# Three small shifts in a hand-written schedule: partial-result stores one slot sooner, the x chunks of block 2 two slots later, the first num burst one slot later

## The chip, the cores and the metric

The kernel runs on one core of a Trainium2 chip. The metric is the device time of one execution in microseconds. Three runs of the kernel before gave 513.34, 508.83 and 507.54 us; the median is 508.83 us.

The core has a matrix engine (PE, whose weight loads are listed as PEld), a vector engine (DVE), a scalar engine (ACT), a general-purpose engine (POOL) and a sync engine (SP), each with its own in-order queue of instructions, and 16 DMA engines that move data between device memory and the on-chip buffers. Nearly all transfers of this kernel are issued from SP's queue.

## The reference

One input x of 2048 rows by 512 feeds two branches, which a gate per row mixes:

```
g   = sigmoid((x * gate_w).sum(-1))
a   = linear attention of x: q, k, v = x @ wqkv, 32 heads of 16
      phi(y) = concat(softmax(y @ w_phi), softmax(-y @ w_phi))    for q and k
      kv = phi(k)^T v,  z = phi(k) summed over the rows
      o  = phi(q) kv / (phi(q) z + 1e-6),  a = o @ wo
b   = relu(x @ w1 + b1)^2 @ w2 + b2                                F = 1792
out = g * a + (1 - g) * b
```

## The kernel before

**Numbers.** Every large product is made of three matmuls on numbers that are split into a high and a low half (names ending in h and l: `xh`, `xl`, `w1h`, `w1l`, `hh`, `hl`, `oh`, `ol`). A split is one copy on ACT, which makes the high half, and one subtraction on DVE, which makes the low half (`split`, L65 to L71). `mm3` (L73 to L77) issues the three matmuls of a product; so L75, L76 and L77 are the lines of nearly all matmuls.

**Two sweeps of the feed-forward branch (FFN).** The rows of x are four blocks of 512. The 14 chunks of the hidden width are done in two sweeps of seven chunks. One step t is one chunk for one block: `do_up(t + 2)` makes 12 matmuls into a bank `u`, ACT and DVE make `hh` and `hl` of it (`hidden`, L453), and `down` makes 12 matmuls that add into the four accumulators `d`. After the seven steps of a block in sweep 0, DVE (L812) turns the four accumulators into four tiles `row`, and SP stores them to `part` in device memory (L817); sweep 1 reads them back and adds its own half.

**The attention branch in the gaps.** In sweep 0 the keys and values are made, two row chunks at a time (tiles `kx`, `ky`, `kz`; p1 to p7), and summed up (`kvps`, `kvs`). In sweep 1 the queries follow (`q`, `q_phi`, `transposed`), then for each pair of row chunks a burst of 32 small matmuls, `numer` (banks `num0`, `num1`, L420), then `attended` (bank `att`), whose matmuls take the split of num (`oh`, `ol`) as an operand.

**The fold of wq.** w_phi is multiplied into wq on the chip: `foldq_load` (slot 16) loads four tiles of wqT into `row` tiles (L200) and w_phi into a stage tile; `fold("q")` (L202) is a burst of 128 small matmuls (L209) in the middle of the `down` of step 9, whose results DVE transposes (L224, into `wqin`) and SP stores (`wqm`, L234). The burst writes four banks in turn: the two `u` banks and the two attention banks, of which one was `kz` (read last by DVE into `vext`) and one was `ky` (read last by DVE into `k`, L564).

**What sets the order.** `at(slot, f)` puts a call into a table; there are two slots to a step. Slot 2t runs ahead of `do_up(t + 2)`, slot 2t + 1 between it and the `down` of step t. A scheduler then orders each engine's queue from that program order, with priorities (`tc.high_priority`) and a few forced orders (`tc.issue_after`); every queue is fixed when the program is built. The pool of `row` tiles has six buffers, which the rows of the partial results, of wqT and of the sums of x (`rows_make`, POOL) share; a tile that takes over a buffer waits until the last user is done with it, for a partial result until its store has landed. On SP each transfer also waits for the one that was issued eight before it on the same queue.

**x.** `x_fetch(b)` loads the four chunks of block b (L161, tiles `xin`), `x_ready(b, k)` splits them (L67 on ACT, L70 on DVE) and `x_save` stores the halves for sweep 1.

Of the kernel before, what the change touches and what calls it, by code (L numbers as in the profile page):

```python
# [37 lines left out]
def tile_gated_mix(ctx: ExitStack, tc: tile.TileContext, xT, xn, wqT, wkT, wphi, wv, wo, w1, b1, w2, b2, gw, out):  # L38
    nc = tc.nc
# [33 lines left out]
    def mm3(o, a, b, sa, sb, first, last, **kw):  # L73
        (ah, al), (bh, bl) = a, b
        nc.tensor.matmul(o, ah[:, sa], bh[:, sb], start=first, stop=False, **kw)  # L75
        nc.tensor.matmul(o, ah[:, sa], bl[:, sb], start=False, stop=False, **kw)  # L76
        return nc.tensor.matmul(o, al[:, sa], bh[:, sb], start=False, stop=last, **kw)  # L77
# [10 lines left out]
    def row():  # L88
        return work.tile([P, D], F32, tag="row", name="row", bufs=6)
# [112 lines left out]
    def fold(nm):  # L202
        wph, t = st["wphi"], st["wT", nm]
        pss = [ps_u.tile([P, 512], F32, tag="u", name=f"fold{nm}{r}") for r in range(2)]
        pss += [p.tile([P, 512], F32, tag="s", name=f"fold{nm}") for p in banks]

        def mm(g, r, q):
            rows, cols = slice(32 * r, 32 * r + 32), slice(g * P + 32 * r, g * P + 32 * r + 32)
            return nc.tensor.matmul(pss[r][32 * q:32 * q + 32, g * P:(g + 1) * P], wph[rows, cols],  # L209
                                    t[g][rows, :].rearrange("r (k q i) -> r k q i", q=4, i=32)[:, :, q, :],  # L210
                                    start=True, stop=True, skip_group_check=True)


        todo = [(g, r, q) for g in range(NK) for q in range(4) for r in range(4)]
        with ExitStack() as stack:
            for i, x in enumerate(todo):
                st["up"] = mm(*x)
                if i < 4:
                    stack.enter_context(tc.issue_after(st["up"].ins))
        w = work.tile([P, 2, 4, NG, 32], F32, tag="phiT", name=f"w{nm}in", bufs=1).rearrange(  # L220
            "p u r g s -> p (u r g s)").rearrange("p (k g r s) -> p k g r s", k=NK, g=NK, r=4)
        for r in range(4):
            with tc.high_priority(offset=AHEAD):
                st["turn"] = nc.vector.transpose(w[:, :, :, r, :].rearrange("p k g s -> p g k s"),  # L224
                                                 pss[r].rearrange("p (g k i) -> p g k i", g=NK, i=32))
        st["w", nm] = [w[:, k].rearrange("p g r s -> p (g r s)") for k in range(NK)]
# [255 lines left out]
    def down(t, c, dps):  # L482
        sw, b, i = work_list[t]
        end = i == NFH - 1 or t == last - 2 and c == NC - 1
        st["down"] = mm3(dps[c], hid[t], down_w[sw * NFH + i], slice(c * P, (c + 1) * P), ALL, i == 0, end)
# [180 lines left out]
    def at(slot, f, *a):  # L666
        steps.setdefault(int(slot), []).append(lambda: f(*a))
# [40 lines left out]
    for b in range(NB):  # L708
        for c in range(NC):
            s = b * SL + 2 * c if b else 7 + c  # L710
            at(s, gate_load, b * NC + c)
            at(s + 2, gate_dot, b * NC + c)
        at(b * SL + 12, gates, b)
        at(b * SL + 15, x_save, b)
        if b < NB - 1:
            at((5, 17, 31)[b], x_fetch, b + 1)
            for k in range(NK):
                at((7, 20, 34)[b] + k // 2, x_ready, b + 1, k)
    base = (NB - 1) * SL
    at(46, foldq_fetch)  # L720
    for k in range(NK):
# [10 lines left out]
    for p in range(NB * NC // 2):  # L732
        n, s = 2 * p, 54 + 6 * p + 2 * (p > 0)
        q, late = divmod(n, NC)[0], p == NB * NC // 2 - 1
        t = s + 12 - late + 2 * (p == 0)
        at(t, finish, n, n % NC)
        at(t + 1, finish, n + 1, n % NC + 1)
        for c in range(2):
            at(s + 2 * c, do_q, NB + q, n + c, n % NC + c)
            at(s + 2 * c + 2 * (p == 0), do_q_scaled, n + c, n % NC + c)  # L740
        at(t - 2, do_n, p)
    for b, slot in enumerate((46, 63, 72, 82)):
        at(slot, do_x, NB + b)

# [3 lines left out]
    def do_up(t):  # L748
        if t < len(work_list):
            sw, b, i = work_list[t]  # L750
            fc = sw * NFH + i
            hid[t] = up(fc, st["x", sw * NB + b], up_w[fc], t == FOLD_AT[0] + LAG)
# [4 lines left out]
    for t, (sw, b, i) in enumerate(work_list):  # L757
        with tc.issue_after(st["turn"].ins) if t == FOLD_AT[0] + 1 else nullcontext():
            for f in steps.get(2 * t, ()):
                f()  # L760


        with tc.issue_after(st["down"].ins) if 0 < t <= LAG else nullcontext():
            fold("k") if t == 1 else do_up(t + LAG)
        for f in steps.get(2 * t + 1, ()):
            f()
        if i == 0:
            dps = [ps_d.tile([P, 512], F32, tag="d", name=f"d{c}") for c in range(NC)]


        now = () if t == last - 1 else (t - 1, t) if t == last else (t,)

        with tc.issue_after(st["up"].ins) if t < LAG else nullcontext():
            for c in range(NC):
                if t == last and c == NC - 1:
                    break
                if t == FOLD_AT[0] and c == NC // 2:
                    with tc.issue_after(st["down"].ins):
                        fold("q")
                    with tc.issue_after(st["turn"].ins):  # L780
                        st["rest"]()
                with tc.issue_after(st["up"].ins) if t == FOLD_AT[0] and c >= NC // 2 else nullcontext():
                    for u in now:
                        down(u, c, dps)
        if t == 1:
            with tc.issue_after(st["down"].ins):
                do_up(t + LAG)
        if t == last:
            ends = [ps_u.tile([P, 512], F32, tag="u", name=f"end{j}") for j in range(2)]
            sc = slice((NC - 1) * P, NC * P)  # L790
            for j, s in enumerate(halves):
                for u in now:
                    st["down"] = mm3(ends[j][:, s], hid[u], down_w[NFH + u - last + NFH - 1], sc, s, u == now[0], u == last)
        if i < NFH - 1:
            continue
        for c in range(NC):
            n = b * NC + c
            done = ("f", n) in st
            if sw == 0:
                o = row()  # L800
                nc.scalar.activation(o, b2b, AF.Copy, scale=rest[:, n:n + 1])
            else:
                if not done:
                    st["f", n] = row()
                    nc.sync.dma_start(st["f", n], part[n])
                o = st["f", n]
            dst = part[n] if sw == 0 else out[n * P:(n + 1) * P, :]
            final = t == last and c == NC - 1
            for d, ss in [(dps[c], (ALL,))] + ([(ends[0], halves[:1]), (ends[1], halves[1:])] if final else []):
                for s in ss:  # L810
                    with tc.high_priority(offset=AHEAD):
                        nc.vector.scalar_tensor_tensor(o[:, s], d[:, s], rest[:, n:n + 1], o[:, s], ALU.mult, ALU.add)  # L812
            if final:
                for e, s in zip((nc.sync, nc.scalar), halves):
                    e.dma_start(dst[:, s], o[:, s])
            elif sw == 0 and b < NB - 1:
                at(2 * t + 3 + c // 2, lambda *a: nc.sync.dma_start(*a), dst, o)  # L817
            elif sw == 0 or done:
                nc.sync.dma_start(dst, o)

# [46 lines left out]
```

## Time and profile before

| | |
|---|---|
| median of three runs | 508.83 us |
| the profiled execution, its own time | 508.95 us |
| its span, first to last instruction | 507.2 us |
| DVE busy | 404.3 us (80%) |
| ACT busy | 254.3 us (50%) |
| POOL busy | 75.5 us (15%) |
| DMA, all queues | 84.79 MB, mean 167 GB/s |
| granted PE clock, mean | 1.000 |

The span is 1.8 us shorter than the execution's own time. A row of the timeline has the start in us from the first instruction, the length in us, the engine, the line of the kernel, the operation, the tile written and the tiles read, and how many instructions were joined into the row; a bracket at its end gives the idle time ahead of it and who ended it. SPq is SP's queue of transfers. In the chain of waits a row has a start, a length and what the end of the kernel waited for in that time.

### The profile page before, as it was taken

To read this page: it belongs to the slowest core of one execution; us is meant where nothing else is said; L and a number is where in the kernel's file an instruction comes from. 1 tells how busy PE (TensorE), PEld (TensorE's weight loads), DVE (VectorE), ACT (ScalarE), POOL (GpSimd) and SP (SyncE) were. 2 spreads that over 40 slices of the span, in tenths; PEclk is the share of its full clock that TensorE was granted. 3 is DMA by queue.
4 is the path that set the end of the run, shared out by engine and by line. 5 is a ranking of instruction groups with operands and counts; after the bars stand their busy time and mean duration, and the time that the engine had idled before them with its cause. 6 is when DMAs were issued, how large, how long until landed. Compare 5 with 4: busy or idle time off the path is not lost.

```text
span 507.2 us, 9518 instructions
## 1 busy us (share of the span) xinstructions
PE 500.7 (99%) x3616; PEld 404.2 (80%) x3616; DVE 404.3 (80%) x642; ACT 254.3 (50%) x433; POOL 75.5 (15%) x77
## 2 busy tenths in 40 slices
PE   9999999899999999999999999999999999999997
PEld 4878888688888888888888878788787878788876
DVE  5979995797879777887889998978789677798724
ACT  6598573454654557273664744343525353433530
POOL 5303020202050000000004131202121212102100
PEclk9999999999999999999999999999999999999999
DMA  8998777886556756936658252223153221032102
GB/s 297 336 359 291 244 261 251 280 300 188 177 199 232 239 175 200 298 111 177 187 161 310 75 191 54 89 52 95 37 179 100 83 79 44 7 101 81 41 23 83
DMA packets 52437, 84.79 MB, mean 167 GB/s; under 512 B 8104, under 2 KB 14504, under 8 KB 52392
## 3 DMA queue, kind: packets, MB, share of 16 engines
q1 hardware_dynamic: 52072, 83.79, 51.2%
q8 instruction: 28, 0.46, 0.4%
q10 hardware_dynamic: 288, 0.39, 0.2%
q14 instruction: 17, 0.14, 0.1%
q0 software_dynamic: 32, 0.01, 0.0%
HBM read 56.37 MB, written 21.50 MB: 154 GB/s over the span
## 4 chain that ended last, share of the span: by engine, by line
PE 94%; ACT 3%; DMA 3%; issue 0%; DVE 0%; SPq 0%
PE u L75 9%; PE d L75 9%; PE d L77 9%; PE d L76 9%; PE u L76 9%; PE u L77 9%; PE q L75 3%; PE q L76 3%; PE att L77 3%; PE q L77 3%; PE att L75 3%; PE att L76 3%; PE ky L75 2%; PE ky L77 2%; PE ky L76 2%; PE kvps L374 2%
## 5 line engine op out<-in xcount | busy, mean ns | idle before, releaser
L455 ACT ACTIVATE r<-u,b1c 128x512 f32<-128x512 f32 x56 | 38.4, 685 | 146.8 <-PE u L77 146.7
L383 POOL TENSOR_TENSOR ez<-e,z 128x512 f32<-128x512 f32 x32 | 41.8, 1328 | 278.2 <-ACT e L354 160.4
L75 PE MATMUL d<-w2h,hh 128*128 128x512 f32 x160 | 62.6, 391 | 0.0
L77 PE MATMUL d<-w2h,hl 128*128 128x512 f32 x160 | 62.3, 389 | 0.0
L76 PE MATMUL d<-w2l,hh 128*128 128x512 f32 x160 | 62.3, 389 | 0.0
L75 PE MATMUL u<-xh,w1h 128*128 128x512 f32 x152 | 59.6, 392 | 0.1
L76 PE MATMUL u<-xl,w1h 128*128 128x512 f32 x152 | 59.2, 389 | 0.0
L77 PE MATMUL u<-xh,w1l 128*128 128x512 f32 x152 | 59.2, 389 | 0.0
L359 DVE TENSOR_REDUCE sm<-e 128x64 f32<-128x1024 f32 x32 | 38.9, 1214 | 19.3 <-ACT e L354 19.3
L460 DVE TENSOR_TENSOR hl<-r,hh 128x512 fp32r<-128x512 f32 x56 | 38.5, 687 | 13.1 <-ACT hh L459 13.1
L407 ACT ACTIVATE phiT<-tb 32x256 f32<-32x256 f32 x64 | 26.5, 413 | 32.1 <-DVE tb L401 31.4
L354 ACT ACTIVATE e<-e 128x1024 f32<-128x1024 f32 x32 | 33.8, 1055 | 12.6 <-DVE e L352 12.3
L459 ACT ACTIVATE hh<-r 128x512 fp32r<-128x512 f32 x56 | 35.3, 630 | 1.5
L456 ACT ACTIVATE r<-r 128x512 f32<-128x512 f32 x56 | 35.2, 629 | 1.3
L75 PEld LDWEIGHTS d<-w2h,hh 128*128 128x128 f32 x160 | 30.0, 188 | 6.6 <-issue 0.4
L77 PEld LDWEIGHTS d<-w2h,hl 128*128 128x128 f32 x160 | 30.0, 188 | 6.3
L76 PEld LDWEIGHTS d<-w2l,hh 128*128 128x128 f32 x160 | 30.0, 188 | 6.2
L272 POOL TENSOR_TENSOR row<-xin 128x256 f32<-128x256 f32 x16 | 17.3, 1089 | 116.6 <-DVE S4ol L70 27.4
L75 PEld LDWEIGHTS u<-xh,w1h 128*128 128x128 f32 x152 | 28.5, 188 | 7.6 <-issue 0.8
L77 PEld LDWEIGHTS u<-xh,w1l 128*128 128x128 f32 x152 | 28.5, 188 | 6.1
L76 PEld LDWEIGHTS u<-xl,w1h 128*128 128x128 f32 x152 | 28.5, 188 | 5.8
L385 DVE TENSOR_REDUCE dz<-ez 128x64 f32<-128x1024 f32 x16 | 19.4, 1210 | 9.4 <-POOL ez L383 9.3
(544 smaller groups left out, 1161.1 us busy)
## 6 DMA issues: line engine op xcount, KB each, us to landing
in<-in_w SPq DMA_DIRECT2D x66, 256.0 KB, 3.3
phiT<-tb SPq DMA_DIRECT2D x192, 32.0 KB, 1.9
w2l<-lkept SPq DMA_DIRECT2D x20, 256.0 KB, 3.2
w1l<-lkept SPq DMA_DIRECT2D x19, 256.0 KB, 4.0
xin<-in_xT SPq DMA_DIRECT2D x16, 256.0 KB, 5.4
xkept<-xh SPq DMA_DIRECT2D x16, 256.0 KB, 4.2
xkept<-xl SPq DMA_DIRECT2D x16, 256.0 KB, 3.7
in<-in_xn SPq DMA_DIRECT2D x16, 256.0 KB, 2.9
```

The source lines that it names most:

```text
L75: nc.tensor.matmul(o, ah[:, sa], bh[:, sb], start=first, stop=False, **kw)
L76: nc.tensor.matmul(o, ah[:, sa], bl[:, sb], start=False, stop=False, **kw)
L77: return nc.tensor.matmul(o, al[:, sa], bh[:, sb], start=False, stop=last, **kw)
L354: nc.scalar.activation(ef, ef, AF.Exp)
L359: nc.vector.tensor_reduce(sm, e3, AX.X, ALU.add)
L383: nc.gpsimd.tensor_tensor(ez[:, hs, :], e3[:, hs, :], zbc[half], ALU.mult)
L385: nc.vector.tensor_reduce(dz, ez, AX.X, ALU.add)
L407: nc.scalar.activation(dst, src, AF.Copy)
L455: nc.scalar.activation(r, ps, AF.Relu, bias=b1c[:, fc:fc + 1])
L456: nc.scalar.activation(r, r, AF.Square)
L459: st["act"] = nc.scalar.activation(hh, r, AF.Copy)
L460: low = lambda: st.update(low=nc.vector.tensor_tensor(hl, r, hh.bitcast(F32), ALU.subtract))
```

## The change

```
--- before
+++ after
@@ -713,9 +713,9 @@
         at(b * SL + 12, gates, b)
         at(b * SL + 15, x_save, b)
         if b < NB - 1:
-            at((5, 17, 31)[b], x_fetch, b + 1)
+            at((5, 19, 31)[b], x_fetch, b + 1)
             for k in range(NK):
-                at((7, 20, 34)[b] + k // 2, x_ready, b + 1, k)
+                at((7, 22, 34)[b] + k // 2, x_ready, b + 1, k)
@@ -738,7 +738,7 @@
-        at(t - 2, do_n, p)
+        at(t - 2 + (p == 0), do_n, p)
@@ -814,7 +814,7 @@
             elif sw == 0 and b < NB - 1:
-                at(2 * t + 3 + c // 2, lambda *a: nc.sync.dma_start(*a), dst, o)
+                at(2 * t + 2 + c // 2, lambda *a: nc.sync.dma_start(*a), dst, o)
```

Nothing is added or left out: the same instructions run in another order. The stores of the partial results of blocks 0 to 2 move one slot up. The loads and splits of block 2 of x move two slots down. The num burst of the first pair moves one slot down, so that on PE it stands behind the 12 matmuls of the next `do_up` (the `u` of step 35) rather than ahead of them; the 12 matmuls of the `down` of step 33 then stand between it and `att`.

On SP's queue, at the end of block 0, where four partial results (`part`) are stored and wqT is loaded for the fold, before:

```order
L817 DMA part<-row 128x512 x3
L85 DMA in<-in_w 128x512
L118 DMA w2l_980<-lkept 128x512
L200 DMA row<-in_wqT 128x512 x3
L85 DMA in<-in_wphi 128x512
L85 DMA in<-in_xn 128x512
L817 DMA part<-row 128x512
L161 DMA xin<-in_xT 128x512 x3
L200 DMA row<-in_wqT 128x512
L161 DMA xin<-in_xT 128x512
```

And now:

```order
L817 DMA part<-row 128x512 x4
L118 DMA w2l_982<-lkept 128x512
L85 DMA in<-in_w 128x512
L200 DMA row<-in_wqT 128x512 x4
L85 DMA in<-in_wphi 128x512
L85 DMA in<-in_xn 128x512
L85 DMA in<-in_w 128x512
L118 DMA w2l_1049<-lkept 128x512
L85 DMA in<-in_w 128x512
L118 DMA w1l_1055<-lkept 128x512
L85 DMA in<-in_xn 128x512
L161 DMA xin<-in_xT 128x512 x4
```

The fourth store, which stood behind the first three loads of wqT, stands with the other three; the four loads of wqT are together; the loads of x (`xin`) stand behind two pairs of weight loads and a second `xn`.

On DVE, shortly ahead of the fold's transposes (L224); `ky` and `kz` are the banks that the fold writes, and L320 is the dot product of a row chunk of x (`in`, loaded as `in_xn`) for the gate:

```order
-L564 TENSOR_TENSOR vext_115<-ky,t_1005 128x32x16
-L320 SCALAR_TENSOR_TENSOR in,lg<-in,gwb 128x512
+L564 TENSOR_TENSOR vext_115<-ky,t_1007 128x32x16
 L564 TENSOR_TENSOR vext_114<-kz,t_900 128x32x16
-L564 TENSOR_TENSOR k_1149<-ky,t_847 128x512
+L320 SCALAR_TENSOR_TENSOR in,lg<-in,gwb 128x512
+L564 TENSOR_TENSOR k_1143<-ky,t_847 128x512
 L224 STREAM_TRANSPOSE wqin<-foldq_1179 128x4x4x32
```

The dot product stood ahead of both reads of the banks; now it stands between them.

On DVE, behind the first num burst; `dz`, `den`, `w` and `e` belong to the features of the next row chunk, `ol` is the low half of num, which `att` waits for, before:

```order
L385 TENSOR_REDUCE dz<-ez 128x64
L70 TENSOR_TENSOR ol<-num_3778,oh 128x512
L70 TENSOR_TENSOR ol<-num_3779,oh 128x512
L387 SCALAR_TENSOR_TENSOR dz<-dz,inv,r 128x64
L460 TENSOR_TENSOR hl<-r,hh 128x512
L390 SCALAR_TENSOR_TENSOR den<-dz,eps 128x32
L391 RECIPROCAL den<-den 128x32
L393 TENSOR_TENSOR w<-r,den 128x64
L365 TENSOR_TENSOR e<-e,w 128x1024
L460 TENSOR_TENSOR hl<-r,hh 128x512
L401 STREAM_TRANSPOSE tb<-e 128x1024
```

And now:

```order
L385 TENSOR_REDUCE dz<-ez 128x64
L460 TENSOR_TENSOR hl<-r,hh 128x512
L387 SCALAR_TENSOR_TENSOR dz<-dz,inv,r 128x64
L390 SCALAR_TENSOR_TENSOR den<-dz,eps 128x32
L391 RECIPROCAL den<-den 128x32
L393 TENSOR_TENSOR w<-r,den 128x64
L365 TENSOR_TENSOR e<-e,w 128x1024
L70 TENSOR_TENSOR ol<-num_3798,oh 128x512
L70 TENSOR_TENSOR ol<-num_3799,oh 128x512
L401 STREAM_TRANSPOSE tb<-e 128x1024
L460 TENSOR_TENSOR hl<-r,hh 128x512
```

The two `ol` moved behind six operations, from `hl` to the product `e` of 128x1024. `att` itself did not move against them: it is still the next thing on PE behind the `down` that follows.

## The prediction

> **What bounds the kernel now.** I read the page first, then the waits of PE, then the chain of waits, then the timeline of each engine around the places where something waits. The first section of the page:
>
> ```profile
> PE 500.7 (99%) x3616; PEld 404.2 (80%) x3616; DVE 404.3 (80%) x642; ACT 254.3 (50%) x433; POOL 75.5 (15%) x77
> ```
>
> All waits of PE in the whole run (line, who was waited for, total, times, longest):
>
> ```profile
> PE foldq L209 <- DMA row<-in_wqT: 2.3, 1, 2.3
> PE warm L496 <- PEq L856: 0.8, 1, 0.8
> ```
>
> So PE is the bound throughout, and the only thing that holds it up after the start is one load of wqT in the middle of the fold. A matmul's bar overlaps the next one's, so I go by starts from here on; with none of PE's work changed, the time moves only by what PE waits for. The chain of waits and PE's timeline show that one wait:
>
> ```profile
> 78.51 7.80 DMA part<-row
> ...
> 86.37 5.44 DMA row<-in_wqT
> ```
>
> ```profile
> 88.02 1.50 PE L209 MATMUL foldq<-row,in 32*32 32x128 f32 x96
> 91.86 0.51 PE L209 MATMUL foldq<-row,in 32*32 32x128 f32 x32 [2.34 <-DMA row<-in_wqT]
> 92.30 0.50 PE L75 MATMUL d<-w2h,hh 128*128 128x512 f32 x1
> ```
>
> Three quarters of the burst ran at once; the last quarter needed the fourth tile of wqT. That load was issued at 86.37, when the fourth partial result had landed and given its buffer free, and landed 5.44 later. The idle time is 2.34; the bars overlap by about 0.27, so an unbroken burst would have gone on up to 2.6 sooner.
>
> **The stores one slot sooner, and x behind the fold.** SP's queue around it:
>
> ```profile
> 72.70 1.64 SPq L817 DMA_DIRECT2D part<-row  x3
> 74.79 0.33 SPq L85 DMA_DIRECT2D in<-in_w  x1
> 75.76 0.32 SPq L118 DMA_DIRECT2D w2l<-lkept  x1
> 76.14 1.37 SPq L200 DMA_DIRECT2D row<-in_wqT  x3
> 77.60 0.38 SPq L85 DMA_DIRECT2D in<-in_wphi  x1
> 78.03 0.42 SPq L85 DMA_DIRECT2D in<-in_xn  x1
> 78.51 0.42 SPq L817 DMA_DIRECT2D part<-row  x1
> 79.03 2.66 SPq L161 DMA_DIRECT2D xin<-in_xT  x3
> ```
>
> DVE finishes the four partial results one after the other, so the fourth store can go some 0.65 behind the third, near 74.7, into a queue that is nearly empty; the weight load `in_w` then waits behind it and behind `w2l`, which is held for PE until 75.76. From there at 0.45 an issue (three in 1.37): `in_w` 76.15, the wqT loads 76.6, 77.05, 77.5 and 77.95, w_phi 78.4, `xn` 78.85. Take for each the worst row, 7.80 from issue to landing: the fourth store lands at 82.5 at the latest, and if it did, the fourth load would follow it as before by 5.44, at 87.9; in the empty queue it lands before 77.95, and the load at 85.75. Both are ahead of 89.3, where the last quarter of the burst would begin; w_phi lands by 86.2, ahead of 88.02. So the wait goes: **-2.5** (from -2.34, the idle time, to -2.6).
>
> What is late next is the start of the burst. It writes the banks `kz` and `ky`, which DVE must have read:
>
> ```profile
> 86.13 0.69 DVE L320 SCALAR_TENSOR_TENSOR in<-in,gwb 128x512 f32<-128x512 f32 x1 [4.14 <-DMA in<-in_xn]
> ...
> 87.35 0.68 DVE L564 TENSOR_TENSOR k<-ky,t 128x512 f32<-128x512 f32 x1
> ```
>
> `k` ended at 88.03 and the burst started at 88.02: it was just in time, behind a dot product that waits for `xn`. Between the two rows stood `vext`, 0.6 of DVE's time; now `vext` stands ahead of the wait, but `xn` is issued 0.8 later (78.85 for 78.03). At the old latency `k` ends at 88.2, and PE waits **+0.2**. Below: nothing, if `xn` is no later than before. Above: +1.4, if `xn` lands two transfers later still (0.65 each, as the three stores follow each other). The Trainium skill's page DMA: Bandwidth & Descriptors (section Anatomy of one DMA) fits a transfer, on the gpsimd path, as 2.0 us plus its bytes at 436 GB/s; by that these 256 KB take an estimated 2.6, `xn` is there at 81.5 and the +0.2 is nothing. The rows have 5.44 and 7.80 in the loaded queue, so the trace does not agree here.
>
> The displaced `in_w` (1.35 later) feeds a copy on ACT, which is idle behind it:
>
> ```profile
> 86.76 0.69 ACT L455 ACTIVATE r<-u,b1c 128x512 f32<-128x512 f32 x1 [8.53 <-PE u L77]
> ```
>
> 8.53 hides it: nothing. The stores of blocks 1 and 2 meet no wait of PE in the list above, so they have none to remove: nothing; what they hold up on SP is one weight load for under a microsecond each.
>
> The loads of x (L161) now stand behind two pairs of weight loads, which go sooner, and behind `xn` of the next chunk, whose buffer the dot product gives free: they are issued from about 87 on, for 79.03 to 86.75 before. They still stand ahead of the stores of `wqm`, whose landing frees the tile that the splits `S` of the next pair take. Before:
>
> ```profile
> 104.83 1.16 ACT L67 ACTIVATE S<-row 128x512 fp32r<-128x512 f32 x2 [4.46 <-DMA wqm<-wqin]
> ```
>
> ```profile
> 113.25 0.68 DVE L70 TENSOR_TENSOR xl<-xin,xh 128x512 fp32r<-128x512 f32 x1
> ```
>
> ```profile
> 116.58 0.39 PE L76 MATMUL u<-xl,w1h 128*128 128x512 f32 x1
> ```
>
> The last low half ended at 113.93 and PE took it at 116.58: 2.65 to spare. With the fold 2.5 sooner, PE wants it near 114.1. The `wqm` stores follow the transposes of the fold, so they too can go 2.5 sooner, and with less ahead of them on SP; ACT, which idled 4.46 for them, gets that back. I carry DVE's queue through at its old durations and get the last low half near 112, some 2 to spare: nothing, up to +2.85 if the stores do not come sooner (rival below).
>
> **The num burst one slot later.** PE at the burst and at `att`, before:
>
> ```profile
> 297.76 1.35 PE L420 MATMUL num<-phiT,kvb 64*32 64x256 f32 x32
> ...
> 304.62 0.39 PE L75 MATMUL att<-wo0h,oh 128*128 128x512 f32 x1
> ```
>
> This burst took 1.35, that of the second pair 1.09:
>
> ```profile
> 326.48 1.09 PE L420 MATMUL num<-phiT,kvb 64*32 64x256 f32 x32
> ```
>
> So up to 0.26 is to be had by moving it away from its data; PE would then reach `att` at 304.36. But `att` needs `ol`, and its cover shrinks from 24 matmuls to 12. DVE, before:
>
> ```profile
> 302.23 1.16 DVE L385 TENSOR_REDUCE dz<-ez 128x64 f32<-128x1024 f32 x1
> 303.31 1.27 DVE L70 TENSOR_TENSOR ol<-num,oh 128x512 fp32r<-128x512 f32 x2
> 304.50 0.28 DVE L387 SCALAR_TENSOR_TENSOR dz<-dz,inv,r 128x64 f32<-128x64 f32 x1
> 304.69 0.69 DVE L460 TENSOR_TENSOR hl<-r,hh 128x512 fp32r<-128x512 f32 x1
> 305.30 0.24 DVE L390 SCALAR_TENSOR_TENSOR den<-dz,eps 128x32 f32<-128x32 f32 x1
> 305.57 0.35 DVE L391 RECIPROCAL den<-den 128x32 f32<-128x32 f32 x1
> 305.96 0.23 DVE L393 TENSOR_TENSOR w<-r,den 128x64 f32<-128x64 f32 x1
> 306.22 1.22 DVE L365 TENSOR_TENSOR e<-e,w 128x1024 f32<-128x1024 f32 x1
> 307.36 0.68 DVE L460 TENSOR_TENSOR hl<-r,hh 128x512 fp32r<-128x512 f32 x1
> ```
>
> DVE runs without a break here, and the first `ol` ended near 303.95, 0.65 ahead of `att`. Now six operations stand ahead of it. By the starts above: 303.31, plus `hl` 0.61, L387 0.30, L390 0.27, L391 0.39, L393 0.26, L365 1.14 is 306.28; `ol` 0.68 makes it 306.96. ACT's `oh` is ready by then: the next `u`, 12 matmuls 0.23 apart, now begins in the burst's place and ends near 300.8; relu, square and copy, and two `oh` with a copy between, six operations of 0.7 at most by ACT's row above, end by 305.0. `att` starts at 307.0 on this clock, where it started at 304.62: **+2.4**, with the 0.26 already used up in it. Bounds: nothing less than -0.26, if `ol` were not waited for; above, +2.8, as DVE's chain itself begins behind POOL's `ez` and can slip some tenths. What waits behind `att` on PE is everything; DVE's own queue waits for nothing in return.
>
> **The sum**, against the profiled execution of 508.95 (span 507.2 and 1.8 around it): -2.5 + 0.2 + 2.4 = +0.1, so 509.0. The profiled execution is 0.1 above the median of 508.83 and I leave that.
>
> **Rivals.**
> 1. *The wait for `ol` is hidden*: `att` at 304.36. For it: the fold's gain leaves every engine but DVE with more room. Against: the queue is fixed, and DVE has no idle time in those rows to work ahead in. 508.95 - 2.5 + 0.2 - 0.26 = 506.4.
> 2. *The chunks of x come too late*, the case on the slow side: if the stores of `wqm`, behind the late loads of x, still land only for 104.83, then ACT's `S`, its weight copies and `xh`, and behind them `e` and DVE's sums run as late as before. Five more operations of 0.6 now stand on DVE ahead of the last low half (`t`, a dot product, `hl` and two other halves, which used to be done sooner), so it ends near 113.93 + 3.0 = 116.95, for 114.1. It decides from about 2 us later than I work out, and costs up to 2.85: 511.9.
> 3. *The change does not free the fold*: the fourth load still lands late, in a queue that is no shorter. Against: it is issued 8 us sooner. 508.95 + 2.4 = 511.4.
> 4. *The wait at `att` lowers PE's clock.* At the start PE took 12 matmuls of 128x512 in 4.96, 0.41 each; later ones follow at 0.23:
>
> ```profile
> 0.78 4.96 PE L496 MATMUL warm<-const-bfloat16-1.0 128*128 128x512 bf16 x12 [0.78 <-PEq L856]
> ```
>
> ```profile
> 9.51 0.40 PE L474 MATMUL u<-xh,w1h 128*128 128x512 f32 x1
> 9.74 0.40 PE L474 MATMUL u<-xl,w1h 128*128 128x512 f32 x1
> ```
>
> If a gap sent PE back to that for as long as at the start, some 8.7 us at little more than half speed, it would lose up to 3.9; 509.0 + 3.9 = 512.9, and for half that time 511. The gap that I work out is 2.5 (304.5 to 307.0). The Trainium skill's page TensorE: Matmul & The Clock Gate (section Why this matters for your kernels) warns of PE gaps of more than about 3 us, after which a window of idle time halves the clock. By that rule 2.5 is safe and 3.2 is not; the trace agrees so far as it goes: after the 2.34 of the fold the next rows follow at once at 0.23 to 0.34.
>
> **How the numbers follow.** My forecast has 0.72, rival 1 0.12, rival 2 0.07, rival 3 0.05, rival 4 0.04. The forecast alone runs from 508.6 (-2.6, 0, +2.4) to 510.6 (-2.34, +1.4, +2.6). To hold 8 in 10 I take in rival 1 below, with a little room for its terms, and leave 2, 3 and 4 out above: 506.2 to 510.8. One per cent, about what a measurement of this kernel can tell from no change, is 5.1 us: faster than 503.7 needs more than the only wait that there is, 0.01; slower than 513.9 needs rivals 2 and 4 in full together, or something that I do not see, 0.03; within it, 0.96.
>
> **What would show each step.** PE's list of waits: the fold's wait on wqT gone; in its place one of about 2.5 on `ol` at the first `att`, with all six operations ahead of it on DVE; at the fold's start at most some tenths on `k`. The four wqT loads issued within 2 us, right behind four stores in one row. The last low half of block 2 done about 2 us ahead of PE. I am wrong if `att` runs through, if the fold still waits, or if PE waits at the first `u` of block 2.

## The result, and the profile after

| | before | after |
|---|---|---|
| median of 22 runs each, us | 507.71 | 511.25 |
| lowest and highest, us | 506.42, 513.34 | 509.33, 512.65 |
| the profiled execution, us | 508.95 | 510.51 |

The changed kernel takes 1.0055 of the time before, 95% interval 1.0038 to 1.0073: some 2.8 us (1.9 to 3.7) slower, which is within the one per cent called no change, as forecast. This ratio, like those below, is that of the means; between the two medians lie 3.5 us. The prediction had 509.0 with a range of 506.2 to 510.8; the median lies 0.45 above the range.

All waits of PE in the profiled execution of the changed kernel (who waited for whom; total, times, longest in us):

```profile
PE att L75 <- DVE ol L70: 2.6, 1, 2.6
PE u L523 <- DMA win<-in_w: 1.0, 1, 1.0
PE warm L496 <- PEq L856: 0.8, 1, 0.8
```

The wait of the fold is gone, one of 2.6 for `ol` has come. The 1.0 at L523 is a wait for a weight load at the kernel's start, ahead of everything that the change touches; the other profiles below show 0 to 0.9 there. The fold's queue and the fold, as timelines of SP and PE:

```profile
73.78 2.29 SPq L817 DMA_DIRECT2D part<-row  x4
...
77.74 1.81 SPq L200 DMA_DIRECT2D row<-in_wqT  x4
```

```profile
89.10 1.94 PE L209 MATMUL foldq<-row,in 32*32 32x128 f32 x128
```

Four stores in one row, four loads of wqT in 1.81 behind them, and all 128 matmuls of the fold without a break. Around `att`, PE and then DVE:

```profile
296.38 0.39 PE L77 MATMUL d<-w211h,hl 128*128 128x512 f32 x1
...
299.42 1.09 PE L420 MATMUL num<-phiT,kvb 64*32 64x256 f32 x32
...
303.07 0.39 PE L77 MATMUL d<-w212h,hl 128*128 128x512 f32 x1
306.06 0.50 PE L75 MATMUL att<-wo0h,oh 128*128 128x512 f32 x1 [2.61 <-DVE ol L70]
```

```profile
302.35 0.68 DVE L460 TENSOR_TENSOR hl<-r,hh 128x512 fp32r<-128x512 f32 x1
302.94 0.28 DVE L387 SCALAR_TENSOR_TENSOR dz<-dz,inv,r 128x64 f32<-128x64 f32 x1
...
304.18 1.22 DVE L365 TENSOR_TENSOR e<-e,w 128x1024 f32<-128x1024 f32 x1
305.33 1.28 DVE L70 TENSOR_TENSOR ol<-num,oh 128x512 fp32r<-128x512 f32 x2
```

The burst takes 1.09 for 1.35, and the six named operations stand ahead of `ol` on DVE, as worked out. What the profile does not show: this execution ran at a mean granted clock of 1.000, but of the 22 runs only 6 did (median 509.8); 16 show 0.997 (median 511.7). The typical run of the changed kernel is not the profiled one.

### The profile page after: what moved, and what is told of

It is laid out like the page before. It is cut to its first block, busy times and chain, and to the rows that moved or that the text cites. A ratio compares the mean times of both kernels' runs of the same rounds, so it can differ in the third digit from the quotient of the medians.

```text
span 508.7 us, 9519 instructions
## 1 busy us (share of the span) xinstructions
PE 501.0 (98%) x3616; PEld 403.7 (79%) x3616; DVE 405.1 (80%) x642; ACT 254.2 (50%) x433; POOL 74.9 (15%) x77
## 4 chain that ended last, share of the span: by engine, by line
PE 96%; DMA 1%; ACT 1%; SPq 0%; DVE 0%; issue 0%
PE u L75 10%; PE d L75 10%; PE d L77 10%; PE d L76 10%; PE u L76 9%; PE u L77 9%; PE att L75 3%; PE q L75 3%; PE q L76 3%; PE att L76 3%; PE att L77 3%; PE q L77 3%; PE ky L75 2%; PE ky L76 2%; PE ky L77 2%; PE kvps L374 2%
```

## The experiments

Theory A is the prediction's sum. Theory B: the new gap at `att` lowers PE's clock for a while (rival 4). Theory C: the fold of the kernel before mostly waits for less than in its profiled execution. Theory D, formed after the first four: the x loads, where they stood, starve PE of instructions. Kernel 1 is the kernel of experiment 1, and so on.

**1. Without the num burst's move.**

```
-        at(t - 2 + (p == 0), do_n, p)
+        at(t - 2, do_n, p)
```

> The changed kernel with the first num burst put back to its old slot; the stores and the x chunks stay moved. Theory A (the prediction's sum: the fold gives 2.5, the wait for `ol` takes 2.4): no wait at the fold, none at `att`, 2.3 to 2.6 us faster than before, ratio 0.995 to 0.9955. Theory B (the gap at `att` also lowers PE's clock, as rival 4 has it, in most executions): the same for this kernel, since it has no gap; the granted clock is 1.0 in every run. Theory C (in most executions of before the fold waits for less than the 2.3 us of its profiled one): no waits either, but only 1.0 to 1.8 us faster, ratio 0.9965 to 0.998. If the gain is nothing, the fold's wait was not worth what the profile shows.

507.19 median of 11, against 508.21 before in the same stretch of runs: ratio 0.9987 (0.9979 to 0.9996). No wait of PE but the one at the very start; clock 1.0 in nine runs, 0.999 in two. The fold's gain is real, but it is 0.7 us by the ratio (0.2 to 1.1) and 1.0 between the medians, and not 2.5: nearer to C than to A, and below what either expected. This is the only kernel here whose whole interval lies below 1.

**2. The num burst alone** (in the kernel before).

```
-        at(t - 2, do_n, p)
+        at(t - 2 + (p == 0), do_n, p)
```

> The kernel before with the first num burst alone one slot later. Theory A: the wait at the fold stays at about 2.3 us, `att` waits about 2.6 us for `ol`, 2.2 to 2.6 us slower than before, ratio 1.0043 to 1.0051, granted clock 1.0. Theory B: granted clock 0.997 in most runs and 1.0 in the others; the runs at 0.997 are 1.5 to 2 us longer than those at 1.0, so 3.5 to 4.5 us slower than before in the median, ratio 1.007 to 1.009. Theory C says nothing of this one.

511.09 median of 8, ratio 1.006 (1.0037 to 1.0084). Five runs at clock 0.997 (median 511.75), three at 1.0 (509.62): the two kinds that B expects, 2.1 apart, though the whole is less than B's 3.5 to 4.5 slower. Its waits:

```profile
PE att L75 <- DVE ol L70: 2.5, 1, 2.5
PE foldq L209 <- DMA row<-in_wqT: 1.1, 1, 1.1
```

The fold, whose program is that of before, waited for 1.1 in this execution: C.

**3. The stores alone** (in the kernel before).

```
-                at(2 * t + 3 + c // 2, lambda *a: nc.sync.dma_start(*a), dst, o)
+                at(2 * t + 2 + c // 2, lambda *a: nc.sync.dma_start(*a), dst, o)
```

> The kernel before with the stores of partial results alone half a step sooner. Theory A: the stores alone free the fourth buffer in time, the wait at the fold is gone and 2.3 to 2.6 us are gained (ratio 0.995 to 0.9955), as without the num burst; the x chunks have no part in it. If the x chunks have a part, this kernel still waits at the fold or at the first u of block 2, and gains less than the kernel without the num burst. Theory C: 1.0 to 1.8 us gained. Theories A, B and C all expect a granted clock of 1.0.

509.02 median of 12, ratio 1.0021 (1.0005 to 1.0036): no gain, a small loss, against all three theories. The timeline of SP and PE:

```profile
77.67 1.80 SPq L200 DMA_DIRECT2D row<-in_wqT  x4
...
80.52 0.69 SPq L161 DMA_DIRECT2D xin<-in_xT  x1
```

```profile
89.03 1.87 PE L209 MATMUL foldq<-row,in 32*32 32x128 f32 x125
92.03 0.41 PE L209 MATMUL foldq<-row,in 32*32 32x128 f32 x3 [1.12 <-issue]
```

The loads of wqT went out as planned, but the burst breaks off three matmuls ahead of its end and waits 1.12 for nothing that the profile names. Since kernel 1, which differs in the place of the x chunks alone, has no such wait, the x chunks have a part in it. Three runs of this kernel are at clock 0.997 or 0.996, though nothing waits at `att`.

**4. `att` later too** (in the changed kernel).

```
-        at(t, finish, n, n % NC)
-        at(t + 1, finish, n + 1, n % NC + 1)
+        at(t + (p == 0), finish, n, n % NC)
+        at(t + 1 + (p == 0), finish, n + 1, n % NC + 1)
```

> The changed kernel with the two att products of the first pair also one slot later, so that 24 matmuls stand between the num burst and `att` as before the change, at 0.23 us each 2.8 us more than in the changed kernel. Theory A: the wait of 2.6 us for `ol` shrinks to 0 to 0.3, the fold's wait stays gone, 2.2 to 2.8 us faster than before. Theory B: the same, and the granted clock is 1.0 in every run, so it is 2.4 us faster than the runs of the changed kernel at clock 1.0 and 4 to 4.5 us faster than those at 0.997. If something other than the gap at `att` lowered the clock (the order of the stores, the num burst by itself), the clock stays 0.997 in most runs here.

510.6 median of 6, ratio 1.0052 (1.0033 to 1.0072): the wait did not go. It moved:

```profile
PE q L75 <- DVE ol L70: 3.1, 1, 3.1
```

With `att` out of the way the next product on PE is `q`, and it writes the bank that `num` still holds until `ol` has read it. So the cover of `ol` cannot be had from `att` alone. Three of six runs at 0.997.

**5 to 7. The gap at `att` made shorter and longer.** In 5, the tail of the other pair's q features (`do_q_scaled` for n = 3) is cut off and put behind `ol`; in 6 more of it, from L387 on; in 7 one `ol` is computed twice.

```
# 5: L365 and the transpose; 6: L387 to L365 and the transpose
+        if n == 3:
+            at(67, do_q_tail, n, c)
+        else:
+            do_q_tail(n, c)
+    def do_q_tail(n, c):
+        with tc.issue_after(st["ol"].ins) if n == 3 else nullcontext():
...
# 7: in numer, for the first pair
+                if "twice" not in st:
+                    st["twice"] = nc.vector.tensor_tensor(ol, pss[r], oh.bitcast(F32), ALU.subtract)
```

> The changed kernel, but the last scaling of the other pair's exponentials (L365 `e`, 1.14 us of DVE ahead of `ol` in the changed kernel) stands behind the two `ol`, while one `hl` (0.6) comes ahead of them: the gap at `att` should shrink from 2.6 to about 2.0. Two forms of theory B. B1 (the clock looks at stretches of fixed length that begin anywhere; a gap that fills enough of one halves the clock for the next; where the stretches fall is chance): a part of the runs still has clock 0.997, fewer than the 21 of 30 that had it with gaps of 2.5 and 2.6. B2 (a threshold near 2.5 us): none has it. If the gap is not the cause of the lower clock, the share stays at about two thirds. Time: 0.6 us under the changed kernel's runs of the same clock, so about 509.2 at clock 1.0.

> The changed kernel, but everything from the scaling of `dz` on (L387 to L365) of the other pair stands behind the two `ol`: the gap at `att` should shrink to about 0.8. B1 and B2: clock 1.0 in all runs, no dip. The gap alone costs then 0.8 less the 0.26 that the num burst gains, so about 507.7, some 0.5 above the changed kernel without the num burst (507.19) and 0.5 under before (508.21). If the clock stays at 0.997 in most runs, the gap is not what lowers it.

> The changed kernel, with the first pair's first `ol` subtraction made a second time behind the two (the same result again, 0.65 us of DVE): the gap at `att` should grow from 2.6 to 3.2 to 3.9. B1 and B2: clock 0.997 or less in all or nearly all runs, against 16 of 22 at 2.6; where the clock is 0.997, 1.6 us are lost behind the gap as in the run that showed it (eight matmuls at 0.43 for 0.23). So 0.65 to 1.3 us above the changed kernel's runs at 0.997: 512.5 to 513.2. If the share of 0.997 stays at two thirds, the length of the gap does not decide it.

5: 509.99 median of 12, ratio 1.0039 (1.0017 to 1.006). 6: 507.85 of 12, ratio 0.9995 (0.9978 to 1.0013). 7: 512.8 of 6, ratio 1.0087 (1.0056 to 1.0118). The gaps in the three profiles, in this order:

```profile
PE att L75 <- DVE ol L70: 2.2, 1, 2.2
```

```profile
PE att L75 <- DVE ol L70: 0.5, 1, 0.5
```

```profile
PE q L75 <- DVE ol L70: 3.1, 1, 3.1
```

In 7 the scheduler put two matmuls of `q` ahead of `att`, so its gap grew to 3.1 and not to 3.9. All runs by the gap of their kernel's profile:

| gap at `att` or `q`, us | kernel | runs | of these at clock 0.997 or less | median at 1.0, at 0.997 or less, us |
|---|---|---|---|---|
| 0 | 1 | 11 | 0 | 507.19, none |
| 0.5 | 6 | 12 | 0 | 507.85, none |
| 2.2 | 5 | 12 | 6 | 509.05, 510.87 |
| 2.5 | 2 | 8 | 5 | 509.62, 511.75 |
| 2.6 | the changed kernel | 22 | 16 | 509.8, 511.7 |
| 3.1 | 4 | 6 | 3 | 509.79, 511.27 |
| 3.1 | 7 | 6 | 6 | none, 512.8 |

In the first two rows the runs at 0.999 are counted with those at 1.0. In two of the six runs of kernel 7 the clock is 0.993. The gap is that of one profile; the two profiles of the changed kernel have 2.6 and 2.5. A gap of 2.2 already lowers the clock in half of the runs, and one of 2.6 leaves it alone in a quarter; the profiles show it directly, with a stretch at half clock behind the 2.23 of kernel 5 and none behind the 2.61 of the changed kernel. That is form B1, not the threshold B2.

The kernels without a gap at `att` that stall at the fold have such runs too, but fewer: 3 of 12 in kernel 3, 2 of 12 in kernel 8 (below), 3 of the 69 runs of the kernel before that were timed beside the experiments. None of these runs was profiled, so what lowered their clock stays open; a longer stall at the fold in them is the obvious candidate.

**8. The traffic of the x loads without their data**, in kernel 1.

```
+    spare = dram.tile([NK, P, D], F32, name="spare")
...
+    at(17, spares)
+    def spares():
+        with tc.issue_after(st["last"].ins):
+            for k in range(NK):
+                nc.sync.dma_start(spare[k], xT[2, :, k, :])
```

> The changed kernel without the moved num burst (507.19, no wait), and in the place on SP's queue where the x chunks of block 2 were loaded before the change, four copies of 256 KB each from the input x to a DRAM tile that nobody reads: the traffic of the old place without its data. Theory D (with the stores alone moved, PE stalled 1.1 us in the fold with all of wqT landed 6 us before, because the x loads keep the DMA engines full from 86 to 92, and PE's own instructions come by DMA): the same stall of about 1 us with no releaser but `issue` is back in the last part of the fold, PE otherwise waits for nothing, and the median is 0.7 to 2.0 above 507.19, near the 509.02 of the kernel with the stores alone. Rival: that stall came from the x tiles (splits that come too soon, buffers) or from chance: then this kernel runs as without the copies, 507.0 to 507.5.

509.36 median of 12, ratio 1.0027 (1.0007 to 1.0047), 2.2 above kernel 1 where 0.7 to 2.0 was expected, and the same break at the same matmul (with a line added above it, L209 is L210):

```profile
88.17 1.87 PE L210 MATMUL foldq<-row,in 32*32 32x128 f32 x125
91.55 0.41 PE L210 MATMUL foldq<-row,in 32*32 32x128 f32 x3 [1.52 <-issue]
```

Two of the twelve runs are at clock 0.997. Traffic alone brings the stall back. What the DMA engines were doing, first in kernel 3, then in kernel 1 (busy time by stretch, with the granted clock, the DMA share and GB/s in the last three columns):

```profile
88.00:90.00 2.00, 2.00 (x79) 1.43 (x82) 0.13 (x1) 1.74 (x3) 0.23 (x1) 1.00 1.07 394
```

```profile
88.00:90.00 2.00, 2.00 (x129) 1.52 (x117) 0.26 (x1) 1.66 (x3) 0.00 (x0) 1.00 0.79 263
```

The engines are full in kernel 3 and not in kernel 1. And instructions come by the same engines. The row of the changed kernel's page (packets, MB, share of the engines) has 28 packets in the whole run, 16 KB each; it does not say for which engine of the core each one is:

```profile
q8 instruction: 28, 0.46, 0.4%
```

Around the fold there is one such packet in every profile. It starts at 89.58 in kernel 3, where PE goes on at 92.03; at 89.21 in kernel 8, where it goes on at 91.55; at 88.11 in a second profile of the kernel before (below), where it goes on at 90.46: 2.3 to 2.5 later each time, always at the 126th matmul. In kernel 1 the packet starts at 87.22, and even there the 126th matmul, at 89.64, comes 0.19 behind the 125th, which is why the burst takes 2.19 there for 1.94 in the changed kernel. In none of the fourteen profiles does that matmul start sooner than 2.3 behind the packet. That the break is a wait for this packet is read from these coincidences; the profile names no releaser. Nor is it shown that only full engines delay it: in the second profile of the kernel before their share is 0.58 from 86 to 88, ahead of the packet.

**9. New profiles of the kernel before and of the changed one, without any edit.**

> The kernel before, profiled once more. Theory A: PE waits 2.2 to 2.5 us for the last load of wqT in the fold, as in its first profile. Theory C: the wait differs from execution to execution and is mostly 1.0 to 1.5 us, as in the kernel with the num burst alone (1.1), whose program is the same up to there; the time is then 0.8 to 1.3 us less than in the first profile, about 507.8.

> The kernel before, a third profile. Theory A: 2.2 to 2.5 us of wait at the fold. Theory C: 1.0 to 1.5, or any value between that and 2.3 if the wait is spread.

The fold in the two new profiles of the kernel before (509.16 and 508.22):

```profile
89.12 1.49 PE L209 MATMUL foldq<-row,in 32*32 32x128 f32 x96
91.84 0.51 PE L209 MATMUL foldq<-row,in 32*32 32x128 f32 x32 [1.23 <-DMA row<-in_wqT]
```

```profile
87.88 1.87 PE L209 MATMUL foldq<-row,in 32*32 32x128 f32 x125
90.46 0.40 PE L209 MATMUL foldq<-row,in 32*32 32x128 f32 x3 [0.71 <-issue]
```

With that of kernel 2, four executions of this program as far as the fold have waited 2.34, 1.09, 1.23 and 0.71 in the fold, 1.34 in the mean: C, with the last of them the stall without a releaser and not the wait for wqT. C's time is missed: the first of the two took 509.16, not some 507.8. In it the load ended the wait at 91.84, almost where it did in the first profile (91.86), but PE came to the fold 1.1 later, so the shorter wait gained nothing: a wait for a transfer takes up whatever lateness PE brings along, which is why its length is not what its removal gains.

> The changed kernel, profiled once more. Theory B: with a chance of about two in three the mean clock is 0.997; then the granted clock is 0.5 for some 3.4 us behind the wait at `att`, about eight matmuls follow at 0.43 instead of 0.23, and the execution takes 1.6 us more than one at clock 1.0 with the same waits. If the lower clock stands elsewhere (at the fold, at the end), theory B falls for this kernel.

512.12, clock 0.997: the other kind of run. PE behind `att`, and the stretches there (engines' busy time; third from the end the granted clock):

```profile
306.03 0.61 PE L75 MATMUL att<-wo0h,oh 128*128 128x512 f32 x1 [2.49 <-DVE ol L70]
306.44 0.63 PE L76 MATMUL att<-wo0l,oh 128*128 128x512 f32 x1
306.87 0.63 PE L77 MATMUL att<-wo0h,ol 128*128 128x512 f32 x1
...
309.43 0.51 PE L77 MATMUL att<-wot,ol 128*128 128x512 f32 x1
309.78 0.39 PE L75 MATMUL att<-wot,oh 128*128 128x512 f32 x1
310.01 0.39 PE L76 MATMUL att<-wok,oh 128*128 128x512 f32 x1
```

```profile
304.00:306.00 2.00, 0.00 (x0) 0.00 (x0) 1.97 (x4) 0.18 (x1) 0.00 (x0) 1.00 0.21 56
306.00:307.00 1.00, 0.97 (x3) 0.76 (x4) 1.00 (x2) 0.00 (x0) 0.00 (x0) 0.64 0.25 66
307.00:308.00 1.00, 1.00 (x4) 0.81 (x3) 1.00 (x2) 0.24 (x1) 0.00 (x0) 0.50 0.19 49
308.00:309.00 1.00, 1.00 (x3) 0.71 (x3) 0.30 (x1) 0.96 (x3) 0.00 (x0) 0.50 0.19 49
309.00:310.00 1.00, 1.00 (x4) 0.83 (x3) 0.00 (x0) 0.45 (x2) 0.00 (x0) 0.66 0.24 62
310.00:311.00 1.00, 1.00 (x6) 0.81 (x5) 0.33 (x1) 0.00 (x0) 0.00 (x0) 1.00 0.14 37
```

Starts 0.43 apart for 0.23, at half the clock, for 3.4 us, then full speed again: some 0.2 lost at each of eight starts, 1.6 in all (nine steps from `att` on take 3.75, for 2.18 in the first profile).

**10. The x chunks alone** (in the kernel before).

```
-            at((5, 17, 31)[b], x_fetch, b + 1)
+            at((5, 19, 31)[b], x_fetch, b + 1)
-                at((7, 20, 34)[b] + k // 2, x_ready, b + 1, k)
+                at((7, 22, 34)[b] + k // 2, x_ready, b + 1, k)
```

> The kernel before with the x chunks of block 2 alone loaded and split one step later. Theory A: the fourth store and the fourth load of wqT stand ahead of the x chunks on SP as before, so the wait for wqT at the fold stays at 1 to 2.3 us and nothing is gained: ratio 0.999 to 1.001. Theory D: the stall without a releaser does not appear, since the x loads are out of the fold; but without the earlier stores there is a wait for wqT in its place. Rival: the x loads take bandwidth from the fourth store or load, the wait shrinks below 0.7, and 0.5 to 1 us is gained.

508.21 median of 11, ratio 1.0013 (0.9989 to 1.0037): no gain. Its profiled execution waits 0.4 for wqT, less than any of before, but it is also the quickest of the 11 (507.16), so what the x chunks do by themselves stays open.

## Why the prediction was right, and where not

- **The fold's wait goes (-2.5)**: right that it goes, and how; the term was mis-sized. It was taken from one execution that had waited longest of the four now seen. Kernel 1 gained 0.7 by the ratio (0.2 to 1.1) and 1.0 between the medians.
- **The fold's start behind `k` (+0.2)**: right. 0 in the first profile of the changed kernel, 0.39 in the second. (Its upper bound, 0.2 and two transfers of 0.65, adds up to 1.5 and not 1.4.)
- **x chunks of block 2 (0)**: as a cost right, though not with 2 us to spare. The low halves came later than I carried them through: the last one ended at 115.15 and PE took it at 115.40, and the one before it PE took as it came, with a tenth lost; DVE and PE of the changed kernel:

```profile
113.86 1.29 DVE L70 TENSOR_TENSOR xl<-xin,xh 128x512 fp32r<-128x512 f32 x2
```

```profile
114.60 0.50 PE L76 MATMUL u<-xl,w1h 128*128 128x512 f32 x1
...
115.40 0.39 PE L76 MATMUL u<-xl,w1h 128*128 128x512 f32 x1
```

  What was off is the idle time of ACT ahead of `S`, which it was to get back. The stores of `wqm` were issued 3.7 sooner (94.52 for 98.20), but ACT still idled 4.16 for their landing, for 4.46 before. `S` started only 1.8 sooner (103.02 for 104.83), and the last low half ended 1.8 ahead of the 116.95 of rival 2 instead of near 112. So rival 2 was nearer than its 0.07 says, and that PE lost next to nothing here was in part luck.

  As a gain the move was missed: without this edit the earlier stores let the x loads out at 80.52, the DMA engines are full through the fold, and a stall that reads as one for instructions takes the place of the one for wqT. The two edits are one: 1.0021 with the stores alone, 1.0013 with x alone, 0.9987 with both. The prediction saw the loads as work of SP and of buffers, never as load on engines that also bring instructions.
- **`att` waits for `ol` (+2.4)**: right. PE idled 2.6 and 2.5, and the burst gave its 0.26 back (1.09 for 1.35). From the last `d` ahead of the burst (or of the `u` that now stands ahead of it) to `att` PE took 7.18 before and 9.68 and 9.56 in the two profiles of the changed kernel: +2.5 and +2.4, with the six operations in the order given. The row that this starts from, before:

```profile
297.44 0.39 PE L77 MATMUL d<-w211h,hl 128*128 128x512 f32 x1
```

- **Rival 4, the clock (0.04)**: this is the step that failed. It happens in 16 of 22 runs and costs 1.6 in the one that was profiled, 1.9 between the medians of the two kinds, under half of the rival's 3.9. I had set it aside, and left it out of the range, because the gap of 2.34 at the fold left the clock alone; that was one execution of something that does not come in every run. The rule of the Trainium skill's page TensorE: Matmul & The Clock Gate (section Why this matters for your kernels), gaps of more than about 3 us, is contradicted in its figure, since 2.2 was enough in half of the runs here; that the clock falls to half agrees.

So the sum, corrected, in the mean: -0.7 for the fold, +2.5 for `att`, and 1.9 in 16 of 22 runs, +1.4: +3.2, against 2.8 (1.9 to 3.7) measured. For the typical run, one with the lower clock, it is -1.0 + 2.5 + 1.9 = +3.4, against 3.5 between the medians. The parts alone, 0.9987 and 1.006, add to 1.0047, inside the interval of the whole. The two errors, a gain some 1.5 too large and a cost of 1.4 set aside, went the same way. The forecast's level was 1.2 above the typical run of before, which by luck hid part of them. The bounds of the forecast have slips of their own, smaller than all this: -2.6, 0 and +2.4 on 508.95 give 508.75 and not 508.6, and the upper end takes +2.6 for `att` where the step gives up to +2.8.

## What to carry to other kernels

A wait for a transfer is worth the wait of a typical execution, not of one profile: take two or three before pricing its removal. In these kernels a gap of PE of 2.2 us or more cost some 1.5 to 2.1 us more behind itself in part of the runs, so compare the granted clock run by run; a gap of 0.5 left it alone in all 12. When transfers are freed to go sooner, ask what else they now cross: here they met, as the traces read, a packet of instructions, and the fix was to hold other loads back.

## What was not expected of the hardware

The stretch at half clock was 3.4 us long in all five profiles that have one (kernels 2, 4, 5, 7 and the second profile of the changed kernel). It began between 0.3 ahead of PE's first matmul behind the gap (kernel 4, 305.1 for 305.37) and 1.0 behind it (kernel 5, 305.5 for 304.47). That fits a check at fixed intervals of 3.4 us whose position against the program is chance, with about 1.9 us of idle time in one interval needed, an estimate from the shares above. A gap longer than 1.9 then escapes only when an edge of the intervals cuts it into two parts that are both under 1.9. The chance of that is (2 x 1.9 - gap) / 3.4, so by this rule a gap of 2.2 would lower the clock in 53% of the runs, one of 2.6 in 65% and one of 3.1 in 79%; measured are 6 of 12, 16 of 22 and 9 of 12. The runs show the shares and the lengths; the rule behind them is argued.

A second surprise is read, not shown: in a burst of 128 small matmuls in some 1.9 us, a packet of 16 KB of instructions that came late held PE up by 0.7 to 1.5 us.
